# Attention and a gated unit on one core: the PSUM banks laid out by hand, maxima taken over two banks at once, and exponentials without a bias operand

## The chip, the cores and the metric

The kernel runs on one core of a Trainium2 chip. A core has TensorE (PE, matrix products into PSUM), VectorE (DVE), ScalarE (ACT, activations), GpSimd (POOL) and SyncE (SP, here the issuer of all transfers). PSUM has eight banks; a matrix product writes into one bank, and an operation of VectorE or ScalarE reads it from there. Time is device microseconds from launch to end, and the median of several runs is compared.

## The reference

Inputs are q, k and v of shape 8 x 8 x 1152 x 64 (batch, heads, rows, width), all float32, and the weights of a gated unit.

```python
q_pool = q.reshape(B, H, S // 2, 2, D).mean(axis=3)            # 576 rows of queries
scores = (1 / sqrt(D)) * q_pool @ k.transpose(0, 1, 3, 2)       # 576 x 1152 for each head
attn = exp(scores - max(scores)); attn /= sum(attn) + 1e-9
x = (attn @ v), heads side by side                              # 8 x 576 x 512
h = relu(x @ w_in); u, g = h[..., :512], h[..., 512:]
g = (g - mean(g)) / sqrt(var(g) + 1e-6)
g = w_spatial @ g + b_spatial                                   # over the 576 rows
return (u * g) @ w_out
```

The answer has to be as exact as float32, so the kernel carries a number as the sum of two float16 parts and takes a product in two or three pieces. w_in and w_out come as float64 and are converted on the chip.

## The kernel before

**Head pairs.** Two heads are handled together, so there are 32 head pairs, four to a batch. For a head pair `prep` (L270) scales and splits q and k: it takes the sum of squares of all of k and all of q (L132 by way of `square_sum`), turns the two sums into powers of two on VectorE (`scales`, L107 to L122: `qkh`, `qks`, `qkr`), computes `esc` (L287), the factor that undoes the scaling inside the exponential, adds the two rows of each pooled query on POOL (L292), and makes the parts of q and k (L135, L138, L302, L304, L305). Seven small transfers on SP then move halves between partitions.

**Maxima.** `maxima` (L317) finds the row maxima of the scores from the high parts alone. The 576 x 2 query rows are 9 tiles of 128, the 1152 keys three pieces of 384: 27 products (L342, and L333 for the tile that has rows of both heads), each into a bank of PSUM, each read by one maximum of VectorE (L348) into `mt`. Then come the maximum of each three (L352), a transposition (L356), the split into two parts (L358, L359) and two transfers into rows of `xq`, so that the later product subtracts the maximum by itself.

**Attention.** `attention` (L500) runs 18 steps. In each, two products (L506, L507) make a bank of 128 keys x 512 query rows of scores, ScalarE takes exp(esc x score + lnp) into `pt` (L512; lnp is a constant column, the logarithm of 64), and for every second step POOL splits 1024 columns (L524). The 64 rows of a head that don't fit in 512 are collected in four "tail" exponentials (L520). Some steps later `values` (L413) multiplies by v (L428, L432, L435) into `o`, and VectorE divides (L407, L408, L443). `tail_values` and `turn_main` bring the results, transposed, into `xg` as two parts (L401, L402).

**The gated unit.** Two batches make a unit (four in all). Its steps: products for the second half of h and their statistics (L582 to L593), a stretch of VectorE work (square root, `normalise`, L618 to L629), products for u (L646), the spatial product (L688 for 512 columns and L689 for the last 64, both in two banks from `bank()`, read by L695 and L698), the split of the gated result (L135, L138) and the last product (L731).

**What sets the order.** All of these are generators. While `attention(i)` runs, after each of its 40 stops a fixed share of a step is given to `maxima(i + 1)` (`MAX_RATE`, 1.0), to the values' preparation, to `prep(i + 2)`, to the conversion of the weights (up to head pair 7) and, once a unit's inputs are there, to the unit (`MOE_RATE`). The last unit runs alone. The recording layer under it may still move instructions: it keeps its own estimate of when buffers come free.

**PSUM.** Four pools hand out the eight banks in turn: three for scores (`pss`), two for maxima, scales, transpositions and tail values (`pm`), one for values (`o`), two for the unit (`pw`). As long as no unit runs, every second product of the maxima takes a bank of `pw`:

```python
if units or (t + n) % 2:
    pm = ps_m.tile([P, 512], F32, name="pm")
else:
    pm = ps_w.tile([P, 512], F32, name="pw")
```

In the last unit `bank()` takes three of five banks from `pss`.

## Time and profile before

| what | value |
|---|---|
| median of 3 runs | 1374.13 us (1368.56 to 1374.2) |
| profiled execution, its own time | 1378.83 us |
| its span, first to last instruction | 1377.1 us |
| granted TensorE clock, mean | 0.967 |
| busy: PE | 1222.1 us (89%) |
| busy: PEld (weight loads, beside PE) | 741.5 us (54%) |
| busy: DVE | 967.1 us (70%) |
| busy: ACT | 970.6 us (70%) |
| busy: POOL | 847.0 us (62%) |

The profile is one execution. A row of a group reads: line, engine, operation, written tile <- read tiles, shape, count | busy time, mean of one in ns | idle time of the engine just before them and what ended it. A row of waits reads: who waited <- for whom: total us, times, longest. A matrix product's end is modelled, so a row of 0.38 us may be followed by the next product after 0.22; starts tell the pace. Averages over the span mix stages with different limits, so the stretches of time matter.

### The profile page before, as it was taken

Reading aid. Unit: us, or ns where it says so; the run is one execution under the profiler, and the core shown is the slowest. Engines: PE = TensorE matmul, PEld = TensorE weight load, DVE = VectorE, ACT = ScalarE, POOL = GpSimd, SP = SyncE. Lnnn points to the kernel's source line nnn. Section 1 sums busy time; section 2 is a strip of 40 time slices with the busy share of each in tenths; the row PEclk is TensorE's granted clock in tenths of the full one; section 3 lists DMA queues with packets and bytes.
Section 4 is the critical chain, followed back from the end, with each engine's and each line's share of the span. In section 5 each row is a group of like instructions: output and inputs, shape, how many; then the busy total and the mean of one; then the engine's idle time right before and its main releaser. Section 6 shows DMA issues by size and latency. Waiting matters only on the chain.

```text
span 1377.1 us, 33478 instructions
## 1 busy us (share of the span) xinstructions
PE 1222.1 (89%) x13696; PEld 741.5 (54%) x13696; DVE 967.1 (70%) x2068; ACT 970.6 (70%) x1632; POOL 847.0 (62%) x492
## 2 busy tenths in 40 slices
...
GB/s 252 166 97 109 94 124 94 128 93 139 113 96 96 79 94 56 62 126 135 96 96 87 51 91 84 74 118 135 104 96 42 47 94 55 28 24 40 8 1 69
DMA packets 56346, 123.77 MB, mean 90 GB/s; under 512 B 8256, under 2 KB 16448, under 8 KB 56192
## 3 DMA queue, kind: packets, MB, share of 16 engines
...
q8 instruction: 107, 1.75, 0.5%
...
## 4 chain that ended last, share of the span: by engine, by line
PE 47%; DVE 25%; ACT 8%; POOL 7%; DMA 7%; issue 4%; SPq 1%; POOLq 0%; ACTq 0%; DVEq 0%
DVE mt L348 7%; PE pss L507 5%; PE pss L506 5%; PE pw L688 5%; POOL pt L524 4%; PE pm L342 4%; PE pw L731 4%; PE pw L646 3%; PE o L435 3%; PE o L428 3%; PE pw L582 3%; ACT pt L512 3%; DMA kq<-in_qT_dram 3%; PE o L432 3%; DVE vv L138 2%
## 5 line engine op out<-in xcount | busy, mean ns | idle before, releaser
L524 POOL TENSOR_TENSOR pt<-pt 128x1024 f16<-128x1024 f32 x288 | 567.8, 1977 | 265.9 <-ACT pt L512 253.8
L512 ACT ACTIVATE pt<-pss,lnp,esc 128x512 f32<-128x512 f32 x576 | 439.4, 776 | 156.7 <-PE pss L507 148.1
L348 DVE TENSOR_REDUCE mt<-pm 128x1 f32<-128x384 f32 x730 | 395.8, 552 | 139.1 <-PE pm L342 119.2
L435 PE MATMUL o<-vp,pt 128*128 128x65 f16 x2304 | 282.8, 198 | 20.2 <-POOL pt L524 19.9
L428 PE MATMUL o<-vp,pt 128*128 128x65 f16 x2304 | 284.8, 196 | 13.0 <-DVE xm L443 12.8
L506 PE MATMUL pss<-qhi,khi 128*128 128x64 f16 (+1 forms) x1152 | 279.6, 294 | 9.1 <-ACT pt L512 8.0
L432 PE MATMUL o<-vp,pt 128*128 128x64 f16 x2304 | 284.5, 196 | 0.0
L507 PE MATMUL pss<-xq,klo 66*128 66x64 f16 (+1 forms) x1152 | 280.6, 295 | 4.1 <-DMA xq<-mr 4.1
L428 PEld LDWEIGHTS <-pt 128*128 128x128 bf16 x2304 | 222.7, 101 | 85.1 <-DVE xm L443 22.0
L432 PEld LDWEIGHTS <-pt 128*128 128x128 bf16 x2304 | 221.6, 100 | 50.7 <-issue 10.5
L342 PE MATMUL pm<-khi,qhi 128*128 128x384 f16 x652 | 217.9, 335 | 32.6 <-DVE mt L348 27.7
L435 PEld LDWEIGHTS <-pt 128*128 128x128 f16 x2304 | 220.7, 100 | 31.6 <-POOL pt L524 24.8
L507 PEld LDWEIGHTS <-klo 66*128 66x128 f16 x1152 | 99.1, 100 | 48.8 <-issue 17.3
L132 ACT ACTIVATE klo<-kq 128x1152 f16<-128x1152 f32 x64 | 74.6, 1166 | 63.7 <-DMA kq<-in_kT_dram 49.4
L506 PEld LDWEIGHTS <-khi 128*128 128x128 f16 x1152 | 103.5, 100 | 27.9 <-issue 12.2
L342 PEld LDWEIGHTS <-qhi 128*128 128x128 f16 x768 | 76.8, 101 | 66.3 <-issue 28.5
L524 POOL TENSOR_TENSOR ptl<-ptl 128x1152 f16<-128x1152 f32 x32 | 71.1, 2221 | 57.9 <-ACT ptl L520 57.9
L305 POOL TENSOR_TENSOR klo<-kq,khi 128x640 f16<-128x640 f32 x64 | 85.1, 1341 | 20.1 <-ACT khi L304 19.8
L520 ACT ACTIVATE ptl<-pss,lnp,esc 128x256 f32<-128x256 f32 (+1 forms) x128 | 75.6, 591 | 24.8 <-PE pss L507 24.2
L264 POOL TENSOR_TENSOR vp<-vt,vp 128x576 f16<-128x576 f32 x64 | 80.6, 1264 | 20.3 <-ACT vp L262 20.3
L582 PE MATMUL pw<-wi_h,xg 128*128 128x512 f16 x240 | 90.1, 382 | 0.0
L731 PE MATMUL pw<-wo_h,vv 128*128 128x512 f16 x216 | 80.3, 381 | 4.7 <-DVE vv L138 4.7
...
## 6 DMA issues: line engine op xcount, KB each, us to landing
...
```

Source lines behind the costliest of these rows:

```text
L305: nc.gpsimd.tensor_sub(KL[:, 0, a:z], k0[:, a:z], khh[:, 1, a:z])
L342: nc.tensor.matmul(pm[:, :W], lhsT=qhl[:, h, c0 : c0 + P], rhs=khh[:, h, n * NB : (n + 1) * NB, :], start=True, stop=True,)
L348: nc.vector.reduce_max(out=mt[:, t, n : n + 1], in_=pm[:, :W], axis=AX.X)
L428: nc.tensor.matmul(o[:, t], lhsT=top[:, cols], rhs=vp[:, D : D + D1], start=c == 0 and t == 0, stop=False, skip_group_check=True,)
L432: nc.tensor.matmul(o[:, t, 0:D], lhsT=top[:, cols], rhs=vp[:, 0:D], start=False, stop=False, skip_group_check=True)
L435: nc.tensor.matmul(o[:, t], lhsT=rst[:, cols], rhs=vp[:, D : D + D1], start=False, stop=c == NC - 1, skip_group_check=True,)
L506: nc.tensor.matmul(o, lhsT=khh[:, h, c, :], rhs=qhl[:, h, q], start=True, stop=False)
L507: nc.tensor.matmul(o, lhsT=KL[0:KR, h, c, :], rhs=X[0:KR, h, q], start=False, stop=True)
L512: nc.scalar.activation(pt, ps, AF.Exp, bias=lnp, scale=esc)
L524: nc.gpsimd.tensor_sub(t.bitcast(F16)[:, :, 0::2], t, t.bitcast(BF16)[:, :, 1::2])
L582: nc.tensor.matmul(ph, lhsT=xa[:, cc, c0 : c0 + P], rhs=wa[:, cc, DH:DF], start=n == 0, stop=n == 3 * NCC - 1,)
L731: nc.tensor.matmul(py, lhsT=ga[:, fc, c0 : c0 + P], rhs=wa[:, fc, :], start=m == 0, stop=m == end - 1)
```

## The change

It does five things.

- PSUM is laid out by hand: three tiles `pss` for scores in turn, `pso` for values, and two tiles of two neighbouring banks, `psm` and `psw`. Everything that took one of two rotating `pm` banks apart from the maxima now takes the first bank of `psm`.
- A maximum of VectorE reads two banks, 2 x 384 columns, into two columns of `mt`: 13 of two and one of a single bank for a head pair instead of 27. Without a unit the pairs alternate between `psm` and `psw`; with one they all use `psm`. `MAX_RATE` is 0.6 instead of 1.0, and a step is now a pair.
- The exponential has no bias operand. Its constant is put into the maximum instead: `lnp` becomes a column for each head pair, computed by a product and a minimum on VectorE (L308, L311 of the new code), and subtracted from `mx` (L374).
- The sum of squares of q is taken from the 576 pooled rows, not from the 1152 rows before pooling; POOL's addition therefore stands ahead of it.
- The conversion of the weights loses one shift (L151 of the old code), since the low word is read as an unsigned number. The spatial product's two banks, always `psw` now, are read by one operation of 576 columns, and multiplied by one or two.

```diff
--- before
+++ after
...
@@ -61,10 +62,24 @@
     wk = ctx.enter_context(tc.tile_pool(name="wk", bufs=2))
     mo = ctx.enter_context(tc.tile_pool(name="mo", bufs=1))
     sm = ctx.enter_context(tc.tile_pool(name="sm", bufs=1))
-    ps_s = ctx.enter_context(tc.tile_pool(name="ps_s", bufs=3, space=PSUM))
-    ps_m = ctx.enter_context(tc.tile_pool(name="ps_m", bufs=2, space=PSUM))
-    ps_o = ctx.enter_context(tc.tile_pool(name="ps_o", bufs=1, space=PSUM))
-    ps_w = ctx.enter_context(tc.tile_pool(name="ps_w", bufs=2, space=PSUM))
+    psum = ctx.enter_context(tc.tile_pool(name="psum", bufs=1, space=PSUM))
+    NB_S = 3
+    pss = [psum.tile([P, MAIN], F32, name=f"pss{j}") for j in range(NB_S)]
+    pso = psum.tile([P, MAIN], F32, name="pso")
+    psm = psum.tile([P, 2, MAIN], F32, name="psm")
+    psw = psum.tile([P, 2, MAIN], F32, name="psw")
+    turns = {"s": 0, "w": 0}
+    def score_bank():
+        turns["s"] += 1
+        return pss[turns["s"] % NB_S]
+    def unit_bank():
+        turns["w"] += 1
+        return psw[:, turns["w"] % 2]
     nc.scalar.preload_act_table_set("natural_log_exp_and_others")
...
@@ -108,9 +121,8 @@
         n = sq.shape[1]
-        pt = ps_m.tile([P, 512], F32, name="pm")
+        pt = psm[:, 0]
         nc.tensor.matmul(pt[:, :n], lhsT=ones, rhs=sq, start=True, stop=True)
-        yield
         h = sm.tile([P, n], I32, name=name + "h", bufs=2)
         s = sm.tile([P, n], I32, name=name + "s", bufs=2)
         r = sm.tile([P, n], I32, name=name + "r", bufs=2)
@@ -120,6 +132,7 @@
         c = float(2 ** 23)
         nc.vector.tensor_scalar(out=s, in0=h, scalar1=-c, scalar2=204 * c, op0=ALU.mult, op1=ALU.add)
         nc.vector.tensor_scalar(out=r, in0=h, scalar1=c, scalar2=50 * c, op0=ALU.mult, op1=ALU.add)
+        yield
         return s.bitcast(F32), r.bitcast(F32)
     def scale_of(sq, name):
@@ -145,12 +158,11 @@
         V = nc.vector
-        lo, hi = src[:, 0::2], src[:, 1::2]
+        lo, hi = src.bitcast(U32)[:, 0::2], src[:, 1::2]
         V.tensor_scalar(out=t1, in0=hi, scalar1=0xFFFFF, scalar2=None, op0=ALU.bitwise_and)
         nc.scalar.activation(dst, t1, AF.Copy, bias=1.0, scale=2.0 ** -20)
-        V.tensor_scalar(out=t2, in0=lo, scalar1=1, scalar2=None, op0=ALU.logical_shift_right)
-        yield
-        V.scalar_tensor_tensor(out=dst, in0=t2, scalar=2.0 ** -51, in1=dst, op0=ALU.mult, op1=ALU.add)
+        yield
+        V.scalar_tensor_tensor(out=dst, in0=lo, scalar=2.0 ** -52, in1=dst, op0=ALU.mult, op1=ALU.add)
         yield
         V.tensor_scalar(out=t1, in0=hi, scalar1=20, scalar2=0x7FF, op0=ALU.logical_shift_right, op1=ALU.bitwise_and)
@@ -278,18 +290,27 @@
         q0, q1 = kq[:, KEYS : KEYS + S], kq[:, KEYS + S :]
         st.update(qhl=qhl, khh=khh, X=X, KL=KL)
+        nc.gpsimd.tensor_add(q0, q0, q1)
         sq = sm.tile([P, 2], F32, name="sq", bufs=2)
-        for j in range(2):
-            square_sum(sq[:, j : j + 1], kq[:, j * KEYS : (j + 1) * KEYS], KL[:, 0].rearrange("p c k -> p (c k)"))
-            yield
+        junk = KL[:, 0].rearrange("p c k -> p (c k)")
+        square_sum(sq[:, 0:1], kq[:, 0:KEYS], junk)
+        yield
+        square_sum(sq[:, 1:2], q0, junk[:, :S])
+        yield
         s, r = yield from scales(sq, "qk")
         esc = sm.tile([P, 1], F32, name="esc", bufs=NSET)
         nc.vector.scalar_tensor_tensor(
             out=esc, in0=r[:, 0:1], scalar=ESC, in1=r[:, 1:2], op0=ALU.mult, op1=ALU.mult
         )
-        st["esc"] = esc
+        lnp = sm.tile([P, 1], F32, name="lnp", bufs=2)
+        nc.vector.scalar_tensor_tensor(
+            out=lnp, in0=s[:, 0:1], scalar=math.log(PEXP) / ESC, in1=s[:, 1:2], op0=ALU.mult, op1=ALU.mult
+        )
+        nc.vector.tensor_scalar_min(lnp, lnp, 2.0 ** 29)
+        st.update(esc=esc, lnp=lnp)
         s_k, s_q = s[:, 0:1], s[:, 1:2]
-        nc.gpsimd.tensor_add(q0, q0, q1)
         yield
         lower, upper = slice(0, D), slice(D, P)
@@ -319,19 +340,19 @@
         qhl, khh, X = st["qhl"], st["khh"], st["X"]
         W = KEYS // 3
         NB = W // P
-        mt = sm.tile([P, NT, 3], F32, name="mt", bufs=2)
-        for t in range(NT):
-            for n in range(3):
-                if units or (t + n) % 2:
-                    pm = ps_m.tile([P, 512], F32, name="pm")
-                else:
-                    pm = ps_w.tile([P, 512], F32, name="pw")
+        mt = sm.tile([P, 3 * NT], F32, name="mt", bufs=2)
+        for j in range(0, 3 * NT, 2):
+            ps = psm if units or j % 4 else psw
+            w = min(2, 3 * NT - j)
+            for x in range(w):
+                t, n = divmod(j + x, 3)
+                pm = ps[:, x, :W]
                 if t == 4:
                     for h in range(2):
                         c0 = MAIN if h == 0 else 0
                         nc.tensor.matmul(
-                            pm[h * TAIL : (h + 1) * TAIL, :W],
+                            pm[h * TAIL : (h + 1) * TAIL],
                             lhsT=qhl[:, h, c0 : c0 + TAIL],
                             rhs=khh[:, h, n * NB : (n + 1) * NB, :],
                             start=True, stop=True,
@@ -340,19 +361,20 @@
                     h = 0 if t < 4 else 1
                     c0 = t * P if t < 4 else TAIL + (t - 5) * P
                     nc.tensor.matmul(
-                        pm[:, :W],
+                        pm,
                         lhsT=qhl[:, h, c0 : c0 + P],
                         rhs=khh[:, h, n * NB : (n + 1) * NB, :],
                         start=True, stop=True,
                     )
-                nc.vector.reduce_max(out=mt[:, t, n : n + 1], in_=pm[:, :W], axis=AX.X)
-                yield
+            nc.vector.reduce_max(out=mt[:, j : j + w], in_=ps[:, :w, :W], axis=AX.X)
+            yield
         yield
         mx = sm.tile([P, NT], F32, name="mx")
-        nc.vector.reduce_max(out=mx, in_=mt, axis=AX.X)
-        yield
-        yield
-        pt = ps_m.tile([P, 512], F32, name="pm")
+        nc.vector.reduce_max(out=mx, in_=mt.rearrange("p (t n) -> p t n", n=3), axis=AX.X)
+        nc.vector.tensor_scalar_sub(mx, mx, st["lnp"])
+        yield
+        yield
+        pt = psm[:, 0]
         nc.tensor.transpose(out=pt[:NT, :P], in_=mx, identity=ident)
         mr = sm.tile([NT, 2, P], F16, name="mr")
         nc.vector.tensor_scalar_mul(mr[:, 0], pt[:NT, :P], 1.0 / MROW)
@@ -376,7 +398,7 @@
     V_RATE = 0.35
     W_RATE = 0.25
     W_AT = 4
-    MAX_RATE = 1.0
+    MAX_RATE = 0.6
     units = []
...
@@ -507,17 +529,17 @@
             nc.tensor.matmul(o, lhsT=KL[0:KR, h, c, :], rhs=X[0:KR, h, q], start=False, stop=True)
         def main_tile(pt, c, h):
-            ps = ps_s.tile([P, MAIN], F32, name="pss")
+            ps = score_bank()
             products(ps, c, h, MAINS[h])
-            nc.scalar.activation(pt, ps, AF.Exp, bias=lnp, scale=esc)
+            nc.scalar.activation(pt, ps, AF.Exp, bias=0.0, scale=esc)
         def tail_tile(h, n):
-            ps = ps_s.tile([P, MAIN], F32, name="pss")
+            ps = score_bank()
             a, z = CUT[n], CUT[n + 1]
             for c in range(a, z):
                 products(ps[:, (c - a) * TAIL : (c - a + 1) * TAIL], c, h, TAILS[h])
             o = ps[:, : (z - a) * TAIL].rearrange("p (c s) -> p c s", s=TAIL)
-            nc.scalar.activation(ptl[:, a:z, h], o, AF.Exp, bias=lnp, scale=esc)
+            nc.scalar.activation(ptl[:, a:z, h], o, AF.Exp, bias=0.0, scale=esc)
         def split(t):
@@ -557,8 +579,8 @@
             turn[0] += 1
             if last and turn[0] % 5 > 1:
-                return ps_s.tile([P, MAIN], F32, name="pss")
-            return ps_w.tile([P, 512], F32, name="pw")
+                return score_bank()
+            return unit_bank()
         xg = x_parts(un)
         xh, xl = xg[:, 0], xg[:, 1]
@@ -681,21 +703,21 @@
                     (vh[:, t0 + j, ls], ws_h[:, j, :]),
                 ]
             terms += [(te[:, e, fs], ws_h[:, 4, :]), (vh[hs, 4, fs], ws_l[hs, 4, :])]
-            pv = bank()
-            pvt = bank()
+            pw = psw.rearrange("p b n -> p (b n)")
             for n, (l, r) in enumerate(terms):
                 fl = dict(start=n == 0, stop=n == len(terms) - 1)
-                nc.tensor.matmul(pv, lhsT=l, rhs=r[:, 0:MAIN], **fl)
-                nc.tensor.matmul(pvt[:, :TAIL], lhsT=l, rhs=r[:, MAIN:S], **fl)
+                nc.tensor.matmul(pw[:, 0:MAIN], lhsT=l, rhs=r[:, 0:MAIN], **fl)
+                nc.tensor.matmul(pw[:, MAIN:S], lhsT=l, rhs=r[:, MAIN:S], **fl)
                 if n % 3 == 2:
                     yield
-            m0, tl0 = (0, MAIN) if e == 0 else (MAIN + P, MAIN + TAIL)
-            gg = wk.tile([P, DH], F32, name="row")
-            for a, n, pz, ba in ((m0, MAIN, pv, 0), (tl0, TAIL, pvt, MAIN)):
-                nc.vector.scalar_tensor_tensor(
-                    out=gg[:, :n], in0=pz[:, :n], scalar=r_v, in1=b_bc[:, ba : ba + n], op0=ALU.mult, op1=ALU.add
-                )
-                nc.vector.tensor_mul(u[:, fc, a : a + n], u[:, fc, a : a + n], gg[:, :n])
+            gg = wk.tile([P, S], F32, name="row")
+            nc.vector.scalar_tensor_tensor(
+                out=gg, in0=pw[:, :S], scalar=r_v, in1=b_bc, op0=ALU.mult, op1=ALU.add
+            )
+            for a, z, x in ((0, S, 0),) if e == 0 else ((0, MAIN, MAIN + P), (MAIN, S, S)):
+                o = u[:, fc, x : x + z - a]
+                nc.vector.tensor_mul(o, o, gg[:, a:z])
             k = 2 * fc + e
             square_sum(gsq[:, k : k + 1], u[:, fc, e * S : (e + 1) * S], gg.bitcast(F16)[:, :S])
             yield
```

How it stands on the engines, at three places. VectorE, the scales of the fifth head pair, prepared among the maxima of the one before (`qk..` are the powers of two, `qhi` the query's second part). Before:

```order
L121 TENSOR_SCALAR qks<-qkh 128x2
L122 TENSOR_SCALAR qkr<-qkh 128x2
L348 TENSOR_REDUCE mt<-pm 128x1
L287 SCALAR_TENSOR_TENSOR esc<-qkr 128x1
L348 TENSOR_REDUCE mt<-pw 128x1
L348 TENSOR_REDUCE mt<-pm 128x1
L138 SCALAR_TENSOR_TENSOR qhi_120<-kq,qks,xq_114 128x576
```

After:

```order
L133 TENSOR_SCALAR qks<-qkh 128x2
L134 TENSOR_SCALAR qkr<-qkh 128x2
L308 SCALAR_TENSOR_TENSOR lnp<-qks 128x1
L302 SCALAR_TENSOR_TENSOR esc<-qkr 128x1
L311 TENSOR_SCALAR lnp<-lnp 128x1
L369 TENSOR_REDUCE mt<-psw 128x2
L424 TENSOR_TENSOR xg<-psm,xg 128x512
L151 SCALAR_TENSOR_TENSOR qhi_115<-kq,qks,xq_109 128x576
L369 TENSOR_REDUCE mt<-psm 128x2
```

Two operations on `lnp` have come in beside `esc`, and the maxima around them write two columns each.

TensorE, in the second unit's spatial product (`vv` its weights) with maxima of another head pair between. Before:

```order
L507 LDWEIGHTS klo_107
L507 MATMUL pss<-xq_113,klo_107 128x512
L342 LDWEIGHTS qhi_120
L342 MATMUL pm<-khi_117,qhi_120 128x384 [waits DVE_49]
L688 LDWEIGHTS vv
L688 MATMUL pw<-ws_h,vv 128x512
L689 LDWEIGHTS vv
L689 MATMUL pw<-ws_h,vv 128x64
```

After:

```order
L710 MATMUL psw<-ws_l,vv 128x512
L711 LDWEIGHTS vv
L711 MATMUL psw<-ws_l,vv 128x64
L710 LDWEIGHTS vv
L710 MATMUL psw<-ws_h,vv 128x512
L363 LDWEIGHTS qhi_115
L363 MATMUL psm<-khi_112,qhi_115 128x384 [waits DVE_49]
L363 LDWEIGHTS qhi_115
L363 MATMUL psm<-khi_112,qhi_115 128x384
L711 LDWEIGHTS vv
L711 MATMUL psw<-ws_h,vv 128x64
```

One product, waiting for a bank that VectorE has left, has become two in a row, of which the first waits for both banks.

TensorE, the last unit, from one group of the spatial product to the next. Before:

```order
L688 LDWEIGHTS te
L688 MATMUL pw<-ws_h,te 128x512
L689 LDWEIGHTS te
L689 MATMUL pss<-ws_h,te 128x64
L688 LDWEIGHTS vv
L688 MATMUL pw<-ws_l,vv 128x512
L689 LDWEIGHTS vv
L689 MATMUL pss<-ws_l,vv 128x64
L688 LDWEIGHTS vv
L688 MATMUL pss<-ws_h,vv 128x512 [waits DVE_49]
L689 LDWEIGHTS vv
L689 MATMUL pss<-ws_h,vv 128x64 [waits DVE_49]
```

After:

```order
L711 LDWEIGHTS te
L711 MATMUL psw<-ws_h,te 128x64
L710 LDWEIGHTS vv
L710 MATMUL psw<-ws_l,vv 128x512
L711 LDWEIGHTS vv
L711 MATMUL psw<-ws_l,vv 128x64
L710 LDWEIGHTS vv
L710 MATMUL psw<-ws_h,vv 128x512 [waits DVE_49]
L711 LDWEIGHTS vv
L711 MATMUL psw<-ws_h,vv 128x64
```

Both kinds wait for VectorE at the group's start; before, the next group's two banks were others than the group's before it, now they are the same two.

11 lines of the change are left out of this document (5 added, 6 removed).

## The prediction

> **What bounds the kernel now.** I read the stages first, then the costliest groups of each, then who waits for whom. Busy time by engine in stretches of the span (PE, PEld, DVE, ACT, POOL, then granted clock):
>
> ```profile
> span 1377.1 us, 33478 instructions
> 48.50:298.00 249.50, 197.61 (x2453) 129.32 (x2453) 221.23 (x395) 188.63 (x317) 188.54 (x103) 0.89 0.38 111
> 298.00:451.00 153.00, 138.68 (x1565) 85.24 (x1564) 116.28 (x267) 124.66 (x216) 104.62 (x61) 0.94 0.36 108
> 405.00:451.00 46.00, 39.97 (x431) 24.11 (x429) 41.19 (x88) 31.65 (x55) 25.61 (x15) 0.93 0.25 74
> 451.00:722.00 271.00, 253.67 (x2993) 156.46 (x2992) 178.21 (x400) 202.09 (x335) 182.19 (x107) 1.00 0.33 94
> 722.00:769.00 47.00, 41.29 (x435) 24.59 (x434) 41.44 (x89) 32.03 (x56) 25.68 (x14) 0.93 0.24 71
> 769.00:1038.00 269.00, 254.23 (x2991) 156.58 (x2990) 176.09 (x399) 201.32 (x334) 182.75 (x108) 0.99 0.33 95
> 1038.00:1083.00 45.00, 38.64 (x431) 23.17 (x430) 41.07 (x89) 30.01 (x51) 24.73 (x14) 0.96 0.21 60
> 1083.00:1237.00 154.00, 146.62 (x1755) 90.32 (x1754) 108.22 (x234) 104.49 (x169) 101.19 (x58) 0.99 0.16 46
> 1237.00:1377.00 140.00, 135.03 (x1036) 69.87 (x1034) 56.64 (x134) 56.47 (x98) 20.19 (x11) 1.00 0.09 31
> ```
>
> Three regimes follow. To 298 us (seven head pairs, then the weights are in) VectorE is the fullest, 221.2 of 249.5 us. From 451 to 1237 us, attention with the gated unit mixed in, TensorE is: 253.7 of 271 us. Around it lie three stretches in which a unit normalises (405 to 451, 722 to 769, 1038 to 1083 us) and VectorE is the fullest again. The last 140 us are the last unit alone, on TensorE. VectorE's groups up to 298 us:
>
> ```profile
> L348 DVE TENSOR_REDUCE mt<-pw 128x1 f32<-128x384 f32 x98 | 53.2, 546 | 7.1 <-PE pw L342 5.8 <-PE pw L333 0.7 <-PE o L428 0.2
> L151 DVE TENSOR_SCALAR vv<-vv 128x512 int32<-128x512 int32 x9 | 12.9, 1438 | 0.1
> L287 DVE SCALAR_TENSOR_TENSOR esc<-qkr x7: 790/1393/1952, 64.9 to 273.6; 128x1 f32<-128x1 f32 x7
> L121 DVE TENSOR_SCALAR qks<-qkh x7: 227/1003/1600, 64.2 to 271.7; 128x2 int32<-128x2 int32 x7
> L122 DVE TENSOR_SCALAR qkr<-qkh x7: 154/155/1337, 64.3 to 272.5; 128x2 int32<-128x2 int32 x7
> ```
>
> (The last three give min/median/max.) One-column operations take 0.15 us or about 1.4, and L122, which needs nothing from its predecessor, follows the slow L121 at 0.155. A slow one waits for something in SBUF, not for its arithmetic; the reductions, which read PSUM, don't show it.
>
> **Part 1: VectorE up to 298 us.** The removed shift of the weights' low words is L151: 9 x 1.438 = -12.9 us there. Reductions, by two sizes and a run of eight without a gap:
>
> ```profile
> L348 DVE TENSOR_REDUCE mt<-pm 128x1 f32<-128x384 f32 x730 | 395.8, 552 | 139.1 <-PE pm L342 119.2 <-PE pm L333 12.1 <-PE pss L506 0.4
> L352 DVE TENSOR_REDUCE mx<-mt 128x9 f32<-128x27 f32 x32 | 5.6, 176 | 0.6
> 227.04 3.81 DVE mt L348 x8
> ```
>
> (552 - 176) / 357 elements is 1.05 ns each, so a pair of banks takes 0.55 + 0.40 = 0.95 us. Alone that saves 0.15 against two of 0.55; in a run, where each costs 0.476, it is 0.88 against 0.95, 0.07. I take 0.12: 13 pairs x 7 head pairs x 0.12 = -11 us. Added for each head pair are the product and minimum for lnp (L308, L311) and the subtraction from mx (L374). The product or esc follows the other as L122 does L121: 0.16. The other two lie between 0.16 (free) and 1.4 (as L287): together 0.5 to 3.0 us; taken 1.6, since L311 needs L308's result, as L287 needed L121's: x 7 = +11. The subtraction also delays the transposition that ends a head pair's maxima, for which TensorE waits now and then:
>
> ```profile
> PE pm L356 <- DVE mx L352: 10.6, 6, 3.7
> ```
>
> (up to 298 us); VectorE being the bound there, that is in the +11 already. Part 1 is **-13 us** (bounds -23 to +2: all free, or 3.0 us and a saving of 0.07). The setup before 48.5 us has three such shifts and the first 27 reductions: **-3**.
>
> The Trainium skill (SBUF — State Buffer, Who interferes with whom) says that a VectorE instruction with two SBUF inputs, or in a two-port mode, is blocked for the length of a GpSimd operation, and that reductions never are. The L287 and L348 rows agree. By that rule each of the three added operations would wait every time, 3 x 1.4 x 7 = 29, and part 1 would come to +5.
>
> **Part 2: ScalarE.** Rows with zero, one and two per-partition operands:
>
> ```profile
> L401 ACT ACTIVATE xg<-pm 128x512 f16<-128x512 f32 x32 | 19.1, 596 | 11.6 <-PE pm L457 11.5
> L590 ACT ACTIVATE vv<-pw,r_h 128x512 f32<-128x512 f32 x30 | 20.5, 684 | 6.3 <-PE pw L582 6.0
> L512 ACT ACTIVATE pt<-pss,lnp,esc 128x512 f32<-128x512 f32 x576 | 439.4, 776 | 156.7 <-PE pss L507 148.1 <-PE o L435 3.9 <-POOL pt L524 1.5
> L132 ACT ACTIVATE klo<-kq 128x1152 f16<-128x1152 f32 x64 | 74.6, 1166 | 63.7 <-DMA kq<-in_kT_dram 49.4 <-DMA kq<-in_qT_dram 8.8 <-DMA khi<-khi 5.5
> L132 ACT ACTIVATE vt<-vt 128x576 f32<-128x576 f32 x64 | 43.2, 677 | 0.3 <-DMA vt<-in_v_dram 0.3
> ```
>
> Each such operand is 0.09 us, so 22 exponentials of a head pair save 2.0 us and the shorter square 1166 - 677 = 0.49: 2.5 us a head pair, 79 in all. ScalarE leads nowhere except in 298 to 451 us (124.7 of 153 with TensorE at a clock of 0.94): four head pairs x 2.5, of which I take **-7** (0 to -10). The pooling add now stands ahead of the query's square, so ScalarE waits for POOL there; before, POOL waited for that square:
>
> ```profile
> POOL kq L292 <- ACT klo L132: 55.6, 12, 13.0
> ACT klo L132 <- DMA kq<-in_kT_dram: 49.4, 20, 4.7
> ```
>
> Two exponentials (1.4 us) stand between the two squares in ScalarE's order and the add takes 1.4, so I take 0; without that cover it is up to 1.4 us a head pair, with the next exponentials queued behind.
>
> **Part 3: one pair of banks instead of two rotating ones (451 to 1237 us).** An undisturbed product and its reduction:
>
> ```profile
> 702.70 0.32 PE L342 MATMUL pm<-khi,qhi 128*128 128x384 f16 x1
> 702.86 0.38 PE L506 MATMUL pss<-qhi,khi 128*128 128x512 f16 x1
> 703.08 0.38 PE L507 MATMUL pss<-xq,klo 66*128 66x512 f16 x1
> 703.06 0.56 DVE L348 TENSOR_REDUCE mt<-pm 128x1 f32<-128x384 f32 x1 [0.62 <-PE pm L342]
> ```
>
> Products start 0.16 us apart after 384 columns and 0.22 after 512. A pair's banks are thus taken for 0.16 + 0.36 + 0.56 + 0.40 = 1.48 us. In the changed order, priced by these starts (0.03 for 64 or 65 columns), the next pair comes after 1.48 us of TensorE's work in the median, 1.33 at the quarter. The rate of 0.6 on 14 pairs and four closing steps takes as many steps of attention (31 of 40) as 1.0 on 27 did, so the pairs can't spread further. There is no second pair of banks in this stretch, so what is missing is TensorE's wait, with scores, values and unit products queued behind it. Summed over this stretch's shortfalls, the tail values and transposes that share the bank included, this gives 35 us if VectorE is always free, 86 if each reduction starts 0.2 us late, 153 at 0.4. VectorE is 66% busy (178.2 of 271), and a pair no longer queues behind its own kind: I take 0.1, 60 us. Waits of TensorE in 451 to 1237 us now:
>
> ```profile
> PE pm L342 <- DVE mt L348: 16.6, 19, 2.2
> PE o L435 <- POOL pt L524: 5.5, 10, 0.7
> PE o L428 <- DVE xm L443: 5.3, 5, 1.4
> PE pw L731 <- DVE vv L138: 4.7, 3, 1.6
> PE pm L333 <- DVE xg L402: 3.7, 2, 1.9
> PE pm L112 <- DVE gt L127: 2.7, 3, 2.4
> PE pm L333 <- DVE qkh L117: 2.4, 2, 1.2
> ```
>
> The pm rows with their shorter fellows make some 30 us, and modelled ends hide about 0.17 (703.02 less the next start 702.86) of each of 30: 36 in all. So +24. The other three rows (15.5 us) wait for ScalarE's, POOL's and VectorE's results that come earlier now: -10 of them. Part 3 is **+14** (-11 to +107).
>
> **Part 4.** The three normalising stretches run at VectorE's pace: 13 pairs x 0.12, twice where a joint evacuation falls in: **-5**. The last unit had five banks for its eight spatial groups; now all use the one pair, and five of them follow with nothing between:
>
> ```profile
> L688 PE MATMUL pss<-ws_h,vv 128*128 128x512 f16 x40 | 13.2, 381 | 0.0
> 1349.39 0.75 DVE L695 SCALAR_TENSOR_TENSOR row<-pw,r_v,b_bc 128x512 f32<-128x512 f32 x1 [1.40 <-PE pss L689]
> ```
>
> Idle before these products was 0.0. Now each waits for the products' end (0.16), the read of 576 columns (0.75 + 64 x 1.05 ns = 0.82) and the hand-over: 1.0 x 5 = **+5**.
>
> **Sum**, against the profiled execution's own 1378.8 us (its span and 1.7 around it): -13 - 3 - 7 + 14 - 5 + 5 = -9, 1370. That execution is 4.7 us above the median of the runs, so in their terms **1365**.
>
> **Rivals.**
> *Cheap pairs.* VectorE finds the reductions at once, the 35 us end of part 3 (-11), free small operations (part 1 at -23), -10 from ScalarE: -23 - 3 - 10 - 11 - 5 + 5 = -47, which is 1327 in the median's terms. For it: VectorE stood idle 139.1 us before reductions. Against: it has other work in most gaps.
> *The pair of banks sets the pace (slower).* One mechanism: a pair's reduction starts behind other VectorE work, TensorE stands before the next pair's first product. At 0.25 us each, between the 86 and 153 above, it costs some 102 us, part 3 is +56 and the sum +33: 1407. From about 0.13 us on (69 us) the whole change loses. For it: 1.48 us needed against 1.48 given, no slack. Against: VectorE starts 13 fewer operations in a head pair, and TensorE's other waits partly fall into the same gaps.
> *The clock.* In 48 to 298 us TensorE is busy 79% and its clock 0.89; in 298 to 451, 91% and 0.94; later, 94% and 0.99 to 1.00. If waits took 451 to 1237 us back to 0.95, some 735 us of busy time would grow by 31: 1396. For it: those rows. Against: a stall of one pair is under 1 us. The Trainium skill (TensorE: Matmul & The Clock Gate, A second HAM failure mode: psum-queue depth-cycling) describes just this, short idling between groups of products that cycle through banks dropping the clock.
> *Nothing moves.* What each engine saves falls where another ends last: 1374.
>
> **Chances.** Forecast 0.48, its own range 1345 to 1385; cheap pairs 0.18; pair of banks 0.23; clock 0.05; nothing 0.06. About 0.5% is what a measurement can tell from no change here: faster is under 1367, slower over 1381. Of the forecast's share 0.30 is faster, 0.12 the same, 0.06 slower. With the rivals: faster 0.30 + 0.18 = 0.48, same 0.12 + 0.06 = 0.18, slower 0.06 + 0.23 + 0.05 = 0.34. Cutting the cheap case and the pair of banks near their middles leaves out a tenth on each side: 1326 to 1408.
>
> **What would show it.** Exponentials at 684 to 690 ns and reductions of 128x2 at 0.95 us; up to 298 us shorter by 10 to 20 us with lnp's rows near 1.4 us; TensorE's waits on mt in 451 to 1237 us near 60 us; five waits of 1 us on row in the last unit. It is wrong if these waits stay under 30 us (then it is faster than said), if they pass 100, or if the clock there falls below 0.97.

## The result: 8% slower

| | before | changed |
|---|---|---|
| median | 1374.16 us | 1483.97 us (1476.57 to 1491.39, 4 runs) |
| ratio, 95% interval | | 1.081 [1.075, 1.087] |
| profiled execution, its span | 1378.83, 1377.1 us | 1476.57, 1474.7 us |
| granted TensorE clock, mean | 0.967 | 0.953 |

The forecast was 1365 us, with a range that ended at 1408. The stages of the changed kernel, cut where the same head pairs begin (busy PE, PEld, DVE, ACT, POOL, then clock):

```profile
0.00:45.40 45.40, 12.36 (x51) 5.78 (x52) 25.15 (x51) 27.40 (x56) 15.64 (x21) 0.91 0.66 219
45.40:288.60 243.20, 192.88 (x2473) 126.97 (x2473) 205.38 (x324) 177.31 (x329) 190.34 (x106) 0.90 0.41 123
288.60:448.30 159.70, 137.80 (x1543) 84.39 (x1542) 119.72 (x222) 114.44 (x210) 103.97 (x60) 0.96 0.32 96
448.30:1327.70 879.40, 779.51 (x8612) 465.57 (x8612) 573.99 (x969) 533.49 (x941) 514.27 (x297) 0.96 0.25 73
1327.70:1474.70 147.00, 135.67 (x1021) 69.75 (x1019) 54.17 (x122) 54.98 (x98) 19.15 (x10) 1.00 0.08 28
```

The same cuts of the kernel before:

```profile
0.00:48.50 48.50, 16.31 (x51) 5.90 (x52) 27.96 (x65) 30.95 (x62) 17.12 (x22) 1.00 0.71 226
298.00:451.30 153.30, 138.98 (x1566) 85.40 (x1565) 116.58 (x268) 124.96 (x216) 104.92 (x61) 0.94 0.36 107
451.30:1236.70 785.40, 733.84 (x8595) 450.78 (x8593) 544.73 (x1208) 569.38 (x942) 515.95 (x297) 0.99 0.28 82
1236.70:1377.10 140.40, 135.33 (x1037) 70.05 (x1035) 56.64 (x134) 56.73 (x98) 20.49 (x11) 1.00 0.09 31
```

Setup is -3.1, the head -6.3 (the prediction shows its row of before, 249.5), pairs 7 to 10 are +6.4, the stretch in which attention and unit are fused +94.0, the last unit +6.6. Nearly everything is in the fourth row. There the products are the same, all other engines are emptier by share of the time, and the clock is 0.96 instead of 0.99; 734 us of busy time at that clock would grow by some 23 (734 x (0.99/0.96 - 1), an estimate), so most of the 94 is standing still.

The single operations cost what was said:

```profile
L534 ACT ACTIVATE pt<-pss,esc 128x512 f32<-128x512 f32 x576 | 389.6, 685 | 231.5 <-PE pss L529 214.9 <-PE pso L457 9.2 <-POOL pt L546 5.5
L369 DVE TENSOR_REDUCE mt<-psm 128x2 f32<-128x768 f32 x347 | 330.7, 953 | 214.0 <-PE psm L363 206.5 <-PE psm L354 7.2
L715 DVE SCALAR_TENSOR_TENSOR row<-psw,r_v,b_bc 128x576 f32<-128x576 f32 x32 | 26.0, 814 | 44.5 <-PE psw L711 44.4
```

But ScalarE stands 214.9 us before exponentials for TensorE, where it was 148.1: the 50 us that quicker exponentials save became waiting. TensorE's own waits from 448 to 1328 us:

```profile
PE psm L363 <- DVE mt L369: 19.7, 22, 1.9
PE psm L354 <- DVE xg L424: 15.1, 12, 2.8
PE psw L710 <- DVE row L715: 14.4, 6, 2.4
PE psw L753 <- ACT row L773: 12.3, 7, 2.6
PE psm L500 <- DVE mt L369: 6.6, 5, 2.6
PE psm L485 <- DVE xg L424: 4.6, 5, 1.9
```

These are the six longest, all for banks of psm and psw; of the ten shorter rows one is not (1.9 us, for pso). Because modelled ends of products hide part of each wait, I also added up, over all products of the stretch at full clock, the time from one start to the next beyond the columns of the product: 146 us against 80 before, of which psm's users have 96 (43.5 before) and the unit's banks 46 (16.6). The expectations below go by these figures. Their size depends on how a column is priced. With each product priced at the clock granted to it, the same count (an estimate from the starts) closes on the whole +94: psm's users +57 (90 instead of 33), the unit's banks +26 (48 instead of 22), value products -13, scores -3, and +26 because the products themselves take longer at the lower clock.

### The profile page after: what moved, and what is told of

Read it like the earlier page. It is cut to its first block, busy times and chain, and to the rows that moved or that the text cites. A ratio compares the mean times of both kernels' runs of the same rounds, so it can differ in the third digit from the quotient of the medians.

```text
span 1474.7 us, 32964 instructions
## 1 busy us (share of the span) xinstructions
PE 1258.2 (85%) x13696; PEld 752.5 (51%) x13696; DVE 978.4 (66%) x1687; ACT 907.6 (62%) x1632; POOL 843.4 (57%) x492
## 4 chain that ended last, share of the span: by engine, by line
PE 43%; DVE 28%; ACT 9%; POOL 8%; DMA 6%; issue 5%; SPq 1%; POOLq 0%; ACTq 0%; DVEq 0%
DVE mt L369 8%; PE psw L710 6%; PE pss L529 5%; PE pss L528 5%; PE psm L363 5%; PE psw L753 4%; POOL pt L546 4%; ACT pt L534 3%; DMA kq<-in_kT_dram 3%; PE psw L668 2%; PE pso L457 2%; PE psw L604 2%; DVE qks L133 2%; PE pso L450 2%; PE pso L454 2%
## 5 line engine op out<-in xcount | busy, mean ns | idle before, releaser
L534 ACT ACTIVATE pt<-pss,esc 128x512 f32<-128x512 f32 x576 | 389.6, 685 | 231.5 <-PE pss L529 214.9
L369 DVE TENSOR_REDUCE mt<-psm 128x2 f32<-128x768 f32 (+1 forms) x379 | 348.4, 919 | 218.9 <-PE psm L363 211.5
L450 PE MATMUL pso<-vp,pt 128*128 128x65 f16 x2304 | 287.1, 197 | 4.9 <-DVE xm L465 4.9
L457 PE MATMUL pso<-vp,pt 128*128 128x65 f16 x2304 | 283.2, 198 | 8.2 <-POOL pt L546 8.1
L454 PE MATMUL pso<-vp,pt 128*128 128x64 f16 x2304 | 285.6, 196 | 0.0
L363 PE MATMUL psm<-khi,qhi 128*128 128x384 f16 x654 | 172.5, 337 | 33.9 <-DVE mt L369 31.6
L710 PE MATMUL psw<-ws_h,vv 128*128 128x512 f16 x256 | 95.9, 387 | 23.2 <-DVE row L715 18.8
L145 ACT ACTIVATE klo<-kq 128x1152 f16<-128x1152 f32 x64 | 59.0, 922 | 70.5 <-POOL kq L293 46.9
L604 PE MATMUL psw<-wi_h,xg 128*128 128x512 f16 x240 | 89.1, 382 | 6.0 <-ACT vv L612 5.9
L753 PE MATMUL psw<-wo_h,vv 128*128 128x512 f16 x216 | 83.3, 390 | 12.5 <-ACT row L773 12.3
L542 ACT ACTIVATE ptl<-pss,esc 128x256 f32<-128x256 f32 (+1 forms) x128 | 64.0, 500 | 42.3 <-PE pss L529 40.6
```

What stands on the lines that cost most here:

```text
L363: nc.tensor.matmul(pm, lhsT=qhl[:, h, c0 : c0 + P], rhs=khh[:, h, n * NB : (n + 1) * NB, :], start=True, stop=True,)
L369: nc.vector.reduce_max(out=mt[:, j : j + w], in_=ps[:, :w, :W], axis=AX.X)
L450: nc.tensor.matmul(o[:, t], lhsT=top[:, cols], rhs=vp[:, D : D + D1], start=c == 0 and t == 0, stop=False, skip_group_check=True,)
L454: nc.tensor.matmul(o[:, t, 0:D], lhsT=top[:, cols], rhs=vp[:, 0:D], start=False, stop=False, skip_group_check=True)
L457: nc.tensor.matmul(o[:, t], lhsT=rst[:, cols], rhs=vp[:, D : D + D1], start=False, stop=c == NC - 1, skip_group_check=True,)
L534: nc.scalar.activation(pt, ps, AF.Exp, bias=0.0, scale=esc)
```

## The experiments

The first theory was the prediction's rival: a pair of maxima holds both banks, and at 1.48 us needed to 1.48 us given TensorE stands before the next pair. All ratios are to the kernel before, on the same chip.

### Four variants of the changed kernel

**Maxima of one bank each**, on two rotating banks, at the old rate:

```diff
-        for j in range(0, 3 * NT, 2):
-            ps = psm if units or j % 4 else psw
+        for t in range(NT):
+            for n in range(3):
+                pm = (max_bank() if units or (t + n) % 2 else unit_bank())[:, :W]   # max_bank: psm[:, turn % 2]
```

> The changed kernel, but each maximum reads one bank again and the two psm banks are handed out in turn to all their users (rate 1.0). Theory 1 (the pair that holds both banks makes TensorE wait in the fused stage, and the gaps lower its clock): the fused stage returns from 879 us to about 790, the whole to 1385 to 1400, TensorE's excess over its work before psm users falls from 96 us to about 44. Theory 2 (the unit's fixed psw banks and joint reads, 46 us of excess against 17 before, do it): under 15 us gained, 1465 to 1480. Theory 3 (POOL's addition ahead of the query's square holds up ScalarE, 47 us of waits): the same, 1470 to 1484.

Measured: 1503.3 us, 1.093 [1.087, 1.098], which no theory had. Without any pair it was slower still, so the pair was not the cause, or not alone.

**A smaller share of steps for the maxima:**

```diff
-    MAX_RATE = 0.6
+    MAX_RATE = 0.5
```

> The changed kernel with MAX_RATE 0.5 instead of 0.6: the 14 pairs spread over 36 of 40 steps instead of 31. Theory 1: the distance of two pairs grows by a fifth, from 1.48 us of TensorE's work to some 1.8, over the 1.53 us that a pair takes; half of the added 52 us of excess goes, 1440 to 1460. Theories 2 and 3: no change, within 6 us of 1484.

Measured: 1496.8 us, 1.088 [1.082, 1.094]: no relief, and some 13 us worse, which no theory had.

**The spatial product's banks and evacuations as before:**

```diff
-            pw = psw.rearrange("p b n -> p (b n)")
+            pv = bank()
+            pvt = bank()
...
-            nc.vector.scalar_tensor_tensor(out=gg, in0=pw[:, :S], scalar=r_v, in1=b_bc, op0=ALU.mult, op1=ALU.add)
+            for a, n, pz, ba in ((m0, MAIN, pv, 0), (tl0, TAIL, pvt, MAIN)):
```

> The changed kernel, but the spatial product takes its two banks from bank() and reads them by two operations each, as before (in the last unit three of five banks are score banks). Theory 1: only the last unit gains, 5 to 7 us, and the fused stage stays within 10 us: 1470 to 1480. Theory 2: 30 to 36 us gained, about 1450.

Measured: 1478.3 us, 1.075 [1.068, 1.081]; its last stage gives back 6 us, the fused one nothing.

**The query's sum of squares over the 1152 rows, POOL's addition behind the scales, as before:**

```diff
-        nc.gpsimd.tensor_add(q0, q0, q1)
-        square_sum(sq[:, 0:1], kq[:, 0:KEYS], junk)
-        square_sum(sq[:, 1:2], q0, junk[:, :S])
+        for j in range(2):
+            square_sum(sq[:, j : j + 1], kq[:, j * KEYS : (j + 1) * KEYS], ...)
...
+        nc.gpsimd.tensor_add(q0, q0, q1)
```

> The changed kernel, but the query's sum of squares is taken of all 1152 rows again and POOL's addition comes after it. Theory 3: the 47 us that ScalarE waits for POOL go, 1440 to 1465. Theories 1 and 2: within 8 us of 1484, either way (ScalarE has 0.5 us more to do in a head pair).

Measured: 1461.0 us, 1.062 [1.055, 1.069], some 23 us better. A part, but 87 us were still unexplained. So I turned round and put single parts of the change into the kernel before.

### One part alone in the kernel before

**The weights' shift removed:**

```diff
-        lo, hi = src[:, 0::2], src[:, 1::2]
+        lo, hi = src.bitcast(U32)[:, 0::2], src[:, 1::2]
-        V.tensor_scalar(out=t2, in0=lo, scalar1=1, scalar2=None, op0=ALU.logical_shift_right)
-        V.scalar_tensor_tensor(out=dst, in0=t2, scalar=2.0 ** -51, in1=dst, op0=ALU.mult, op1=ALU.add)
+        V.scalar_tensor_tensor(out=dst, in0=lo, scalar=2.0 ** -52, in1=dst, op0=ALU.mult, op1=ALU.add)
```

> The kernel before with one edit alone: the weights' shift is taken out (the low words are read as unsigned and added with the scale 2^-52). Theory L (the PSUM tiles laid out by hand cost the time) and theory X (the folded exponentials cost it) both give this edit its price from the prediction, -12.9 us, since the stretch up to 298 us is VectorE's: about 1361. Above 1372 says that VectorE's gain there is given back behind.

Measured: 1367.9 us, 0.997 [0.995, 0.999]. The head (249.5 us in the prediction's row) is now

```profile
48.90:286.90 238.00, 190.76 (x2451) 124.87 (x2451) 209.38 (x386) 188.45 (x317) 186.79 (x103) 0.92 0.39 117
```

and of these 11.5 us 4.8 are left between the medians; the profiled execution of before is itself 4.7 above its median.

**The pooled query norm** (the last diff the other way round, in the kernel before):

> The kernel before with one edit alone: the two query rows are pooled first on GpSimd and the query's sum of squares runs over the pooled 576 elements. Theories L and X both: undoing it in the changed kernel gained 23 us, so alone it should cost about as much, 1390 to 1400, because the add now stands at the head of the preparation and holds the sum of squares behind GpSimd's exponential subtractions. A rival, that it costs only where PSUM is laid out by hand, expects 1365 to 1375.

Measured: 1396.0 us, 1.018 [1.016, 1.020]. ScalarE's waits show a row that the kernel before doesn't have:

```profile
ACT klo L132 <- POOL kq L282: 40.7, 25, 3.6
```

1.3 us a head pair, with exponentials queued behind it on ScalarE.

**The folded exponentials:**

```diff
+        lnp = sm.tile([P, 1], F32, name="lnp", bufs=2)      # a product and a minimum for each head pair
...
+        nc.vector.tensor_scalar_sub(mx, mx, st["lnp"])
...
-            nc.scalar.activation(pt, ps, AF.Exp, bias=lnp, scale=esc)
+            nc.scalar.activation(pt, ps, AF.Exp, bias=0.0, scale=esc)
```

> The kernel before with one edit alone: the exponentials carry no bias operand, and the constant goes through lnp into the maxima. Theory X: the fold is what costs the fused stage its time (two more small VectorE operations per head pair that wait for GpSimd, and one in the chain maxima to X rows, or exponentials so quick that GpSimd and the clock fall behind), so 1420 to 1460. Theory L: 1350 to 1375, since the exponentials save 90 ns each and ScalarE sets only the stretch 298 to 451 us.

Measured: 1390.4 us, 1.014 [1.012, 1.016], between the ranges of the two theories: the fold costs time, but not the 94 us. The subtraction and TensorE's wait for its result:

```profile
L356 DVE TENSOR_SCALAR mx<-mx,lnp 128x9 f32<-128x9 f32 x32 | 21.5, 673 | 0.4
PE pm L360 <- DVE mx L356: 23.9, 12, 5.6
```

That wait was

```profile
PE pm L356 <- DVE mx L352: 13.4, 9, 3.7
```

before. These 10.5 us more may be so much of the 18; what the rest is isn't settled. Pairs 7 to 10 took

```profile
300.20:458.00 157.80, 137.11 (x1544) 84.20 (x1543) 121.29 (x271) 116.79 (x213) 104.81 (x60) 0.96 0.33 97
```

ScalarE's busy time fell there from 125.0 to 116.8 us and the stretch grew from 153.3 to 157.8: what ScalarE saved became waiting for products (24.5 us instead of 12.9).

**The PSUM layout**, with one bank for each maximum as before. psm and psw are tiles of two banks whose halves take turns:

```diff
-    ps_m = ctx.enter_context(tc.tile_pool(name="ps_m", bufs=2, space=PSUM))
+    psm = psum.tile([P, 2, MAIN], F32, name="psm")       # users take psm[:, turn % 2]
```

(In this one kernel a sum of squares can be overwritten in its bank before the scales are worked out from it, so these are other numbers; the later runs read it at once.)

> The kernel before with one edit alone: the four PSUM pools become tiles that are allocated once and rotate in the same numbers of banks (3, 2, 2 and 1), each maxima operation still reading one bank at the rate 1.0. Theory L: the same banks as fixed tiles lead to another order of the instructions or to coarser waits, 1420 to 1460. Theory X: within 0.5% of 1374.

Measured: 1476.0 us, 1.076 [1.073, 1.078]. Same number of banks, the same products and readers, and 100 us more. That was the main part.

### The same banks, cut into other tiles

In that run a product started before the reduction of the *other* bank had ended in 1% of the cases in the fused stretch; in the kernel before 61% did. So the new theory: the recording layer puts the wait on the tile, not on the bank.

```diff
-    psm = psum.tile([P, 2, MAIN], F32, name="psm")
-    psw = psum.tile([P, 2, MAIN], F32, name="psw")
+    psm = [psum.tile([P, MAIN], F32, name=f"psm{j}") for j in range(2)]
+    psw = [psum.tile([P, MAIN], F32, name=f"psw{j}") for j in range(2)]
```

**A tile for each bank:**

> The kernel before with tiles that are allocated once, as in the run of the layout alone, but every bank is a tile of its own (psm0, psm1, psw0, psw1 in place of the two-bank tiles psm and psw), and the sum of squares is read from its bank before another step is taken. Theory W (a product into one bank of a two-bank tile waits until the reader of the other bank is done, since the waits go by the tile): 1366 to 1384, and the next maxima product starts before the end of the last reduction in over half of the cases in the fused stage, as in the kernel before. Theory F (tiles that are allocated once cost the time however they are cut): 1455 to 1485, and almost none starts before it.

**Two banks to a tile, else the same:**

> The same as the kernel with every bank a tile of its own, sum of squares read at once included, but with the two-bank tiles psm and psw in place of four one-bank tiles. Theory W: 1465 to 1485, the whole distance from 1361 being the waits for the other bank's reader; next products start before the last reduction's end in almost no case. If the step at which the sum of squares is read made the 115 us between the two layouts: 1355 to 1375.

**Only the step at which the sum of squares is read, in the kernel before:**

```diff
         nc.tensor.matmul(pt[:, :n], lhsT=ones, rhs=sq, start=True, stop=True)
-        yield
...
+        yield
         return s.bitcast(F32), r.bitcast(F32)
```

> The kernel before with one edit: the sum of squares is read from its bank by VectorE before another step of the recording is taken. If this edit is what made the layout with a tile for each bank faster than the kernel before: 1358 to 1366. If it was the rotation of tiles that are allocated once: 1370 to 1378.

Measured: a tile for each bank 1361.2 us, 0.992 [0.990, 0.994]; two banks to a tile 1503.5 us, 1.095 [1.092, 1.097]; the reading step alone 1372.7 us, 1.000 [0.999, 1.002]. So 142 us hang on nothing but where the tiles are cut. The two times lie 5 us below and 18 above theory W's ranges; the direction and the overlap are as it said. Fused stretch, two banks to a tile, then the groups of its maxima:

```profile
473.40:1363.50 890.10, 793.84 (x8609) 469.36 (x8608) 610.69 (x1204) 574.21 (x944) 510.87 (x296) 0.96 0.25 73
L364 DVE TENSOR_REDUCE mt<-psm 128x1 f32<-128x384 f32 x730 | 404.6, 554 | 231.8 <-PE psm L358 190.1 <-PE psm L349 39.1
```

A tile for each bank:

```profile
438.20:1217.80 779.60, 735.49 (x8596) 453.40 (x8595) 539.97 (x1208) 570.86 (x942) 518.35 (x297) 0.98 0.28 82
L364 DVE TENSOR_REDUCE mt<-psm 128x1 f32<-128x384 f32 x730 | 395.7, 551 | 140.5 <-PE psm L358 121.9 <-PE psm L349 10.6 <-PE psw L349 0.9
```

How it looks in order of time, two banks to a tile:

```profile
731.97 0.56 DVE L364 TENSOR_REDUCE mt<-psm 128x1 f32<-128x384 f32 x1 [0.68 <-PE psm L358]
732.58 0.32 PE L358 MATMUL psm<-khi,qhi 128*128 128x384 f16 x1
732.94 0.56 DVE L364 TENSOR_REDUCE mt<-psm 128x1 f32<-128x384 f32 x1 [0.41 <-PE psm L358]
...
733.38 0.19 PE L448 MATMUL pso<-vp,pt 128*128 128x64 f16 x1
733.55 0.32 PE L358 MATMUL psm<-khi,qhi 128*128 128x384 f16 x1
...
733.91 0.56 DVE L364 TENSOR_REDUCE mt<-psm 128x1 f32<-128x384 f32 x1 [0.41 <-PE psm L358]
```

Each product starts 0.05 us after the end of the last reduction, although it writes the other bank: 0.36 from its start to the reduction, 0.56 of reduction, 0.05 of hand-over, a maximum every 0.97 us at best, with VectorE idle for 0.41 in each. TensorE is through with the value products (0.03 apart) and stands from 733.41 to 733.55. With a tile for each bank:

```profile
724.41 0.32 PE L358 MATMUL psm<-khi,qhi 128*128 128x384 f16 x1
724.77 1.53 DVE L364 TENSOR_REDUCE mt<-psm 128x1 f32<-128x384 f32 x3 [0.26 <-PE psm L358]
724.88 0.32 PE L358 MATMUL psm<-khi,qhi 128*128 128x384 f16 x1
725.38 0.32 PE L358 MATMUL psm<-khi,qhi 128*128 128x384 f16 x1
```

(x3 are three reductions without a gap, in one row.) Products run beside them. 59% of the products start before the last reduction's end, against 1%. This also says why taking the pair out of the changed kernel had not helped: there, too, both banks of psm were one tile.

### The pair of maxima and the units' banks

A pair needs a tile of two banks, so its price is separate from that of the cut.

**The changed kernel with the units' banks as two tiles** (and the spatial product evacuated bank by bank):

```diff
+    def part():                          # called before the first unit
+        wide.close()                     # the pool that holds psw for pairs of maxima
+        psu.extend(p.tile([P, MAIN], F32, name=f"psu{j}") for j in range(2))
...
-        return psw[:, turns["w"] % 2]
+        return psu[turns["w"] % 2]
...
-            ps = psm if units or j % 4 else psw
+            ps = psm if psu or j % 4 else psw
```

> The changed kernel with one difference: from the first gated unit on, the two banks of the units are two tiles (the spatial product is evacuated bank by bank, as before), and the maxima keep their two-bank tile psm; up to then psw is one tile for pairs of maxima. Theory W: the waits of the units' products, 46 us in the fused stage against 16.6 before, go back by some 25, and the last unit's 5 go too: 1445 to 1460. What is left above 1410 is then the maxima pair's own. Theory F: 1470 to 1485.

**The changed kernel with a tile for each bank and no pairs** (the first edit of this study, on one-bank tiles, and the spatial product bank by bank):

> The changed kernel with every bank a tile of its own: maxima read one bank each at the rate 1.0 and rotate over psm0 and psm1 with the other users, the spatial product is evacuated bank by bank. The fold, the pooled query norm and the missing shift stay. Theory W: the 100 us of the layout go, and what is left is about the sum of the three edits as measured alone (+23, +18 and -5): 1395 to 1420, against 1503 where the two banks of psm were one tile. Theory F: 1480 or more.

**The kernel before with the pairs alone** (the layout with parted unit banks, pairs at the rate 0.6; bias operand, query norm and shift as before):

> The kernel before with the pairs of maxima of the changed kernel (one two-bank tile psm for all its users, rate 0.6, psw as a tile for pairs up to the first gated unit and as two tiles behind it), without the fold, the pooled query norm and the missing shift, and with the spatial product as before. Theory W with the pair as a wait of its own: 1400 to 1435, since the changed kernel with these banks took 1459 and the fold, the pooled norm and the shift measured alone make +23, +18 and -5 of it. If the pair costs only together with the fold and the pooled norm: 1360 to 1385.

**The same, and its control with a tile for each bank, with short maxima.** Each maximum reads 96 of 384 columns, so three quarters of the maxima are left out:

```diff
-            nc.vector.reduce_max(out=mt[:, j : j + w], in_=ps[:, :w, :W], axis=AX.X)
+            nc.vector.reduce_max(out=mt[:, j : j + w], in_=ps[:, :w, : W // 4], axis=AX.X)
```

> The kernel with the pairs of maxima alone, but each maxima operation reads the first 96 of the 384 columns of each bank (three quarters of the maxima are left out; the products stay), so that VectorE holds the pair's tile for about half as long. Theory P (the time that a reduction holds both banks is what the pair costs): the 80 us between the pair and the layout with a tile for each bank shrink to 40 or less against the same shortening there, 1380 to 1400. Theory Q (the other users hold the two banks: transposes that ScalarE and then VectorE read, scales, tails): 1415 to 1440, 60 us or more above it.

> The control: the kernel before with every bank a tile of its own, each maxima operation reading 96 of 384 columns. Both theories: VectorE loses some 0.3 us in each of 864 operations, which counts up to 298 us only, so 1330 to 1358; what the pair costs with short operations is the distance from here.

Measured: units' banks apart 1459.1 us, 1.061 [1.057, 1.064]; all banks apart 1395.5 us, 1.015 [1.013, 1.018]; the pair alone 1441.2 us, 1.049 [1.047, 1.052]; with short maxima 1366.6 us, 0.996 [0.994, 0.998], its control 1361.6 us, 0.989 [0.983, 0.995]. The fused stretch of the pair alone, then with short maxima and the group of its reductions:

```profile
460.20:1300.70 840.50, 765.77 (x8625) 460.49 (x8624) 558.47 (x947) 573.92 (x942) 517.81 (x298) 0.97 0.26 77
```

```profile
441.40:1225.80 784.40, 734.80 (x8596) 453.28 (x8595) 367.80 (x947) 572.24 (x942) 515.05 (x297) 0.99 0.28 82
L371 DVE TENSOR_REDUCE mt<-psm 128x2 f32<-128x192 f32 x353 | 125.0, 354 | 253.7 <-PE psm L365 235.2 <-PE psm L356 14.2 <-PE pss L530 1.7
```

With a reduction of 0.95 us the pair costs 80 us against the layout with a tile for each bank (1441 - 1361). Of these, 61 lie in the fused stretch (840.5 against 779.6) and some 22 before it. With a reduction of 0.35 us it costs 5 (1366.6 - 1361.6, less than the control's own spread of 1348 to 1366), and nothing in the fused stretch (784.4 against 786.5); theory P had expected some of the cost to stay. The hold is then 0.36 + 0.16 + 0.35 = 0.87 us instead of 1.48 (medians in the traces: 0.88 and 1.48), well under the 1.48 that the order leaves between pairs, and the clock is back at 0.99. So the length of the reduction that holds both banks decides what the pair costs.

The transpositions that share the pair have a part in it. TensorE's waits in the fused stretch, the pair alone (two rows), with short maxima, and a tile for each bank:

```profile
PE psm L356 <- DVE xg L425: 27.3, 14, 3.1
PE psm L365 <- DVE mt L371: 7.4, 14, 0.9
PE psm L356 <- DVE xg L425: 15.5, 14, 2.3
PE psm L349 <- DVE xg L418: 4.9, 3, 1.9
```

The longest row of the pair alone is that of maxima products that wait until VectorE has read a transposition (xg) out of the shared tile. It becomes shorter with the reductions, but doesn't go. How much of the 80 us goes through it was not separated.

Shortening VectorE's operations without the pair left the whole time where it was (1361.2 and 1361.6, where 1330 to 1358 was expected). In the head it took 61 us of work off VectorE (153.1 us busy instead of 214.0), and the head became only 8.5 us shorter; pairs 7 to 10 and the fused stretch gave that back (single executions). So it isn't VectorE's work as such that the pair saves or costs.

### A version that beats both

**Pairs only in the head**, where no unit needs the banks, with the shift removed:

```diff
+                elif n == 0:
+                    both = ps_2.tile([P, 2, 512], F32, name="p2")     # until the first unit
...
+                elif n == 1:
+                    nc.vector.reduce_max(out=mt[:, t, 0:2], in_=both[:, :, :W], axis=AX.X)
```

> The kernel before with its pools, without the weights' shift, and with pairs of maxima only up to the first gated unit: there the first two maxima of each row tile go into one two-bank tile on the units' banks, which nobody else uses yet, and one operation reads both; the third keeps a bank of its own. Then the two banks become two tiles again. Of 27 reductions of a head pair 18 become 9 that are cheaper together by about 0.25 us each, 2.3 us a head pair where VectorE sets the time: eight head pairs less 12 to 18 us, with the shift's 5 about 1352 to 1360. If the single pair tile makes VectorE wait for its two products: 1364 to 1375.

Measured: 1369.7 us, 0.997 [0.995, 0.999], no better than the shift alone. In the head (from the first exponential to the eighth pair's) VectorE is 11.1 us less busy than with the shift alone,

```profile
47.80:288.80 241.00, 190.61 (x2452) 125.56 (x2452) 198.25 (x323) 188.77 (x319) 188.49 (x105) 0.91 0.39 115
```

and the seven pairs aren't shorter (241.0 against 238.0 us). VectorE waited there for products of the maxima for 22.0 us instead of 13.1, the second case of the expectation. Whether the single pair tile made it wait, or VectorE had stopped being what sets this stretch, isn't told apart by this run.

**A tile for each bank, and the shift removed:**

> The kernel before with every bank a tile of its own that is allocated once, and without the weights' shift. The two edits gave 0.9916 and 0.9968 alone; if they add: 0.985 to 0.990, 1353 to 1360. If the shift's gain is again given back behind the head: 0.990 to 0.993.

Measured: **1356.7 us, 0.989 [0.988, 0.990]**. The two gains add, and this is the fastest version that was run.

## Why the prediction was wrong

The medians make a chain from the changed kernel to this one: 1484.0; units' banks apart 1459.1 (-25); no pair, every bank apart 1395.5 (-64); without the fold and the pooled norm 1356.7 (-39, where alone they cost 18 and 23). The fused stretch alone goes 879.4, 867.7, 797.3, 781.2 us. In the other direction, the kernel before is at 1374 and lies 13 above the layout by banks and 5 above the removed shift.

- **Part 3, the step that failed.** It took "one pair of banks instead of two rotating ones" to cost +24 of waits less 10, "+14 (-11 to +107)". The pair alone makes this stretch 55 us longer (840.5 against 785.4) and the whole kernel 69. Its mechanism was right (banks taken for 1.48 us, the next pair after 1.48), and so was the rival "the pair of banks sets the pace" with its slack of nothing; the size was wrong. Between its sums of 35 and 86 us it chose 60, for reductions that start 0.1 us late. In the changed kernel psm's reductions started 0.20 us late on average (two thirds of them as soon as their products were through, one in ten 0.8 us or more after), and by the count from starts psm's users waited 90 us, close to its own sum of 86 for 0.2 us. What it took off was about right: the two rotating banks had 33 us of waits for its 36, and the other products' relief came, 13 for its 10. So the waits for psm are +57 where the sum had +24, and most of the rest of the +94 stands in two terms that it had at nothing, the tiles and the clock. (The chain above parts the same stretch by edits instead: 12 for the units' banks, 70 for the pair, 16 for the fold and the norm.)
- **A term that was missing.** The layout as such was priced at nothing: banks were counted and the tiles weren't. psw as one tile makes a unit's product wait for the evacuation of the one before, though it writes the other bank; with the units' banks apart the fused stretch is 867.7 instead of 879.4 us and the last stage 138.7 instead of 147.0. (The count from starts puts +26 of the fused stretch on these banks; 12 of it came back.) The sum had only the 5 of the last unit, and these are there, in five waits of the changed kernel from 1327 us on:

```profile
PE psw L710 <- DVE row L715: 4.4, 5, 1.0
```

  A two-bank tile without any pair costs 142.
- **Part 2** took 0 for the pooled norm, "without that cover it is up to 1.4 us a head pair". The cover was not there: 1.3 us a head pair of waiting, +23 in all instead of 0. And the exponentials' saving of 7 us in pairs 7 to 10 did not come. The stretch is 4.5 us longer with the fold alone, 6.5 with the pooled norm alone and 6.4 in the changed kernel: ScalarE, though fullest for its share, waited for products there.
- **Part 1** had the prices right:

```profile
L308 DVE SCALAR_TENSOR_TENSOR lnp<-qks 128x1 f32<-128x1 f32 x32 | 36.6, 1144 | 0.0
L374 DVE TENSOR_SCALAR mx<-mx,lnp 128x9 f32<-128x9 f32 x32 | 23.1, 723 | 0.9
```

  with the minimum at 0.15 these make 2.0 us a head pair for 1.6 (the dearer case beside the sum, three waits of 1.4 us, did not come, since the minimum didn't wait), the pairs take 0.95 and the shift is gone; but the head gave -6.3 instead of -13. The single edits make -11.5 (shift), +4.1 (pooled norm) and +1.1 (fold) there, which is -6.3 with nothing left for the reductions' -11; single executions differ by some 4 us in this stretch (245.3 with the reading step alone). VectorE was the fullest engine of the head without being what set it: 61 us less work made it 8.5 us shorter. The fold's price on TensorE (its transposition behind `mx`) was called "in the +11 already", and over the whole run it is 10 us more.
- **The clock** was at nothing in the sum too. It went from 0.99 to 0.96 in the fused stretch and was at 0.98 and 0.99 where the waits were gone; an estimated 23 to 26 of the 94 us came by it. That the waits bring it down is not shown. In pairs 7 to 10 it rose from 0.94 to 0.96 while the stretch grew by 6.4 us, and the first layout run, 78 us longer in the fused stretch than the kernel before, had 0.98:

```profile
469.90:1332.90 863.00, 778.35 (x8606) 465.46 (x8605) 569.29 (x1204) 575.61 (x943) 511.81 (x296) 0.98 0.26 75
```

  The Trainium skill (TensorE: Matmul & The Clock Gate, A second HAM failure mode: psum-queue depth-cycling) describes a kernel in which short idling of TensorE between groups of products, with the PSUM banks used in turn, makes the clock swing. The 0.96 here goes that way, the 0.98 of the first layout run doesn't. I had given the clock 0.05 as a cause by itself; here it came on top of another.
- **Setup, last unit.** The setup's -3.1 for -3 is luck. The forecast had it from the shifts and the first reductions, but with the shift alone the setup is 48.9 us, against 48.5 before, and with the pooled norm alone it is 45.4, all of the gain. The last stage is +6.6 for +5, with the five waits that were forecast. The normalising stretches were not measured by themselves.
- **Its signs.** TensorE's waits on mt in the fused stretch make 34 us in the view, between the 30 and 100 that it allowed, though the stretch lost 94: the waits for other readers of psm and for psw were left out of that sign. The sign on the clock, below 0.97, came.

The range ended at 1408 because the bound of part 3 was cut in its middle. Its own upper bound, +107, with the losses of the fold and the norm beside it, would have contained the result (1365 + 93 + 41 = 1499, an estimate).
